# Two key tiles per attention cycle, value sums in SBUF, tiles turned by VectorE: a change to a fused attention and SwiGLU kernel

## The chip, the cores and the metric

The kernel runs on one core of one Trainium2 chip. The metric is device time in microseconds (us) of one execution; the median of several executions is compared. Beside the runs there is one profiled execution, whose trace gives the start and length of every instruction on the engines: PE (TensorE matmul), PEld (TensorE weight load), DVE (VectorE), ACT (ScalarE), POOL (GpSimd) and SP (SyncE, whose queue issues nearly all DMAs here).

## The reference

Two layers with the same weights; in each, an attention block and a feed-forward block are added to x. All values are float32; S = 2048 rows, D = 448, 16 query heads of 28 that share one key head and one value head, F = 1792.

```python
def _A_ref(x, wq, wk, wv, wo):            # H = 16, Dh = 28
    q = (x @ wq).reshape(B, S, H, Dh).transpose(0, 2, 1, 3)
    k = x @ wk                            # (B, S, 28)
    v = x @ wv
    scores = jnp.einsum("bhqd,bkd->bhqk", q, k) * (Dh ** -0.5)
    p = softmax(scores, axis=-1)
    o = jnp.einsum("bhqk,bkd->bhqd", p, v)
    return o.transpose(0, 2, 1, 3).reshape(B, S, H * Dh) @ wo

def _B_ref(x, w_gate, w_up, w_down):
    return (silu(x @ w_gate) * (x @ w_up)) @ w_down

for layer in range(2):
    x = x + _A_ref(_layernorm(x), wq, wk, wv, wo)
    x = x + _B_ref(_layernorm(x), w_gate, w_up, w_down)
```

## The kernel before, in words

**Data.** x stays in SBUF (`xres`, 16 tiles of 128 rows). The 2048 rows form four chunks of 512 (`c` = 0 to 3). Operands of the projections and of the feed-forward are split into a high and a low part in a rounded float32 (`split`, lines 133 to 135, on GpSimd), and products are summed in passes: high by high, low by high, high by low.

**Norm and transposes.** `norm_steps` (L210) gives one chunk's statistics and normalised tiles `xn` (L229 on VectorE; L230 copies the last 64 columns once more with GpSimd). `flip` (L241) turns four tiles at a time with TensorE transposes (L246); `flipped` takes them from PSUM: a copy (L252) and VectorE's subtraction (L253) into `xh` and `xl`. The last 64 of the 448 rows of the turned chunk stand twice, in both halves of the partitions. `rows3` (L128) loads weights in the same layout: one DMA for 384 rows, one that broadcasts the last 64 rows to both halves (L131).

**Projections.** 16 steps per layer (`project`, `q`): chunk by chunk, in each the four groups of columns in the order `TURN` = (3, 2, 0, 1) (L32). Groups 3 and 2 carry the keys in columns 112 to 127 and groups 0 and 1 the values; the queries go to DRAM and come back as stacked heads (`stack`, `parts`, `rows`: `qstack`). For the values VectorE turns the rows (L505) and GpSimd distributes them (`vsb`). In layer 0 the three first groups' `rows` DMAs (L323) are issued at step 13.

**Attention.** There are 16 groups per layer: a chunk of queries by four heads. For each group, 16 steps of one key tile (128 keys) each. `step(n)` (L557): 12 score matmuls (L565), three passes of four heads; heads 0 to 2 go into a tile of three banks (`threes[n % 2]`, two in turn), head 3 into bank 7 (`one`). ScalarE takes the exponential of `one` (L571) and then of the three banks (L572). Then TensorE does the value matmuls of the tile two steps earlier (`pv(n - 2)`, L602), which are summed in bank 6 over all 16 tiles; the ones column of `vsb` gives the row sums. At the end of a group, `post` (L610), called four steps after its last tile: VectorE copies bank 6 to SBUF (L615), four DMAs spread the row sums (`rs`, L618), and some steps later `rest` checks them (L624, L626), takes the reciprocal, sends it through DRAM (`rd`) back as a broadcast (`rb`), and GpSimd multiplies (L636) and splits into `onh`, `onl`. All engines keep the order in which the program is written.

**Between steps.** When a chunk's four groups are done, its out-projection follows in step 10 of a later group (`between_steps`, L575): 48 matmuls (L549) into the free tile of three banks and bank 7, and VectorE's sums into `xres`. In groups 8 and 12 chunk 0's transposes lie between them. In groups 5, 13 and 14 the norm of chunks 0, 1 and 2 is done one piece per step. The feed-forward's first weights are loaded during groups 11 to 13 (`weights`), with `rows3` too.

**Feed-forward.** 14 tiles of 128 columns of F, two at a time (`groups`, FG = 2); for each pair all four chunks. `unit` (L791) does gate and up (L292, 64-row matmuls side by side), ScalarE's silu (L825), VectorE's product (L826), the split of h (L827, L830), and in the next unit the down products, whose sums go to `xres` at the pair's end (`accumulate`, L743 on GpSimd). `rest` (L856) opens it: `turned(1)` flips chunk 1 on TensorE before the first unit of the second chunk, and `self.mid` puts the flips of chunks 2 and 3 into the middle of later units. Steps in `soon` are done so many units later. At the end of layer 0 the chunks are handed to layer 1's projections.

**The second version.** The program holds a second, safer version of everything (`full`), behind a branch that is taken only where row sums leave a range (`fine`). The profiled execution does not take it.

Of the kernel before, what the change touches and what calls it, by code (L numbers as in the profile page):

```python
# [8 lines left out]
F32 = mybir.dt.float32  # L9
# [6 lines left out]
P = 128  # L16
S = 2048
D = 448
# [13 lines left out]
TURN = (3, 2, 0, 1)  # L32
IDLE = 36
# [21 lines left out]
def forward(  # L55
# [72 lines left out]
    def rows3(dst, src, eng=nc.sync):  # L128
        n = src.shape[1]
        eng.dma_start(dst[:, 0:3], src[0:384, :].rearrange("(k p) n -> p k n", p=P))  # L130
        eng.dma_start(dst[:, 3], src[384:448, :][None].to_broadcast([2, 64, n]))  # L131
# [78 lines left out]
    def norm_steps(c, pool=pers):  # L210
# [14 lines left out]
        def apply(t):  # L225
# [4 lines left out]
            nc.gpsimd.tensor_copy(got["x"][:, t, D:512], o[:, 384:D])  # L230
# [18 lines left out]
    def flipped(tiles, k, pt, copy):  # L249
# [12 lines left out]
        nc.vector.tensor_tensor(xh[64:128, k, :], pt[64:128, :], high, ALU.subtract)  # L262

# [39 lines left out]
    class Attention:  # L303


        def __init__(self, layer):
# [3 lines left out]
            self.order = [(c, m) for c in range(NC) for m in TURN]  # L310
# [8 lines left out]
            for i in range(3):  # L319
                self.at(4 + 3 * i, lambda i=i: self.stack(i))  # L320
                self.at(6 + 3 * i, lambda i=i: self.parts(i))
                if not full:
                    self.at(13, lambda i=i: self.rows(i))  # L323
# [137 lines left out]
        def project(self):  # L461
# [5 lines left out]
            turned = [o[0] for o in self.order[self.seen : self.seen + 2] if o[1] == 3]  # L467
# [60 lines left out]
        def scores(self, ff):  # L528
            next(switch)
            with tc.tile_pool(name=f"at{self.layer}", bufs=1, reuse_waits="tile") as wp:  # L530
# [26 lines left out]
                def step(n):  # L557

                    i, kt = divmod(n, NT)
                    three, one = threes[n % 2], banks[7]  # L560
# [8 lines left out]
                    pt = wp.tile([P, 3, 512], F32, name="pt", bufs=3)  # L569
                    pt1 = wp.tile([P, 512], F32, name="pt1", bufs=2 if full else 3)  # L570
                    nc.scalar.activation(pt1, one, AF.Exp, scale=SCALE)  # L571
                    nc.scalar.activation(pt, three, AF.Exp, scale=SCALE)  # L572
                    pts[n] = [*(pt[:, j, :] for j in range(3)), pt1]

                def between_steps(n):  # L575

                    i, kt = divmod(n, NT)
                    free, one = threes[(n + 1) % 2], banks[7]
                    if full:
                        self.lent = free[:, 0, :]  # L580
                        self.advance(KC)
                        if kt == 11 and i + 1 < len(GR):
                            self.places[i + 1](free[:, 1, :])
                    if not todo or kt != 10:
                        return
                    c = todo.pop()
                    ks = list({8: (0, 1), 12: (2, 3)}.get(i, ()))
                    adds = []
                    for t in (1, 2, 3):
                        adds.append(outproj(c, t, free[:, t - 1, :]))  # L590
                        if ks:
                            flip(got, X0, [ks.pop(0)], one)
# [4 lines left out]
                def pv(n):  # L597
                    i, kt = divmod(n, NT)
                    if kt == 0:
                        accs[i] = banks[6]  # L600
                    for j in range(4):
                        nc.tensor.matmul(  # L602
                            accs[i][32 * j : 32 * j + 32, :], vsb[:, kt, :], pts[n][j],
                            start=(kt == 0), stop=(kt == NT - 1), skip_group_check=True,
                        )
                    del pts[n]
                    if kt == NT - 1:
                        due[n + 4] = post(i)

                def post(i):  # L610

                    c, g = GR[i]
                    out2 = halves("o2").bitcast(F32)
                    oraw, rb = out2[:, 0, :], out2[:, 1, :]
                    nc.vector.tensor_copy(oraw, accs.pop(i))  # L615
# [28 lines left out]
                fs, got = norm_steps(0)  # L644
                fs1, got1 = norm_steps(1)
                ff.norms[1] = got1
                ff.second = norm_steps(2)
                last = NT * len(GR)
                for n in range(last):
# [319 lines left out]
```

## Time and profile before

| | us |
|---|---|
| runs | 2038.59, 2038.96, 2035.05 (median 2038.59) |
| profiled execution | 2040.6 |
| its span in the trace | 2038.9 |
| mean granted TensorE clock | 0.996 of full speed |
| layer 0: start and projections | 0 to 72 |
| layer 0: attention (first to last exponentials) | 73 to 595 |
| layer 0: feed-forward | 596 to 1040 |
| layer 1: last projections | 1040 to 1081 |
| layer 1: attention | 1081 to 1600 |
| layer 1: feed-forward | 1601 to 2039 |

Busy time of the engines over the span:

```profile
PE 2015.1 (99%) x18613; PEld 1271.5 (62%) x18613; DVE 457.7 (22%) x890; ACT 1310.6 (64%) x2152; POOL 537.7 (26%) x601
PE   8999999999999999999999999999999999999998
ACT  3699798997973333333348997979979533333332
```

The first row gives each engine's busy time, its share of the span and the number of instructions. The other two cut the span into 40 slices of 51 us; each digit is the busy share of a slice in tenths. PE is busy in all of them. Matmuls are pipelined and their ends are modelled, so a busy PE is not PE at its peak: within attention it also waits for ScalarE and VectorE in ways that the busy share does not tell, and starts of instructions have to be read. ScalarE is near its limit in the two stretches of attention (slices 3 to 12 and 22 to 32, apart from those where the out-projections lie) and at a third elsewhere.

In the lines that follow, an instruction is given as start, length, engine, line, operation, tiles, shape and count; square brackets hold the idle time of the engine before it and what ended that.

### The profile page before, as it was taken

The page shows a single profiled execution, that of the slowest core. Times are in us where ns is not written, and L with a number is a line of the kernel's source. Part 1 is how long each engine was busy: PE and PEld are TensorE (multiplying, and loading weights), DVE is VectorE, ACT ScalarE, POOL GpSimd, SP SyncE. Part 2 cuts the span into 40 slices and gives each one's busy share as a digit, 9 for nine tenths or more (in the row PEclk, how much of TensorE's full clock was granted, in tenths as well). Part 3 has the DMA queues.
Part 4 walks back from the last instruction along what each step waited for, and adds up shares of the span by engine and source line. Part 5 has one row for each costly group of instructions (what it writes and reads, how often), then busy time and mean ns, then how long its engine had stood idle before and what let it go on. Part 6 is the DMA issues. An engine that isn't in the chain of part 4 may idle for free.

```text
span 2038.9 us, 43612 instructions
## 1 busy us (share of the span) xinstructions
PE 2015.1 (99%) x18613; PEld 1271.5 (62%) x18613; DVE 457.7 (22%) x890; ACT 1310.6 (64%) x2152; POOL 537.7 (26%) x601
## 2 busy tenths in 40 slices
PE   8999999999999999999999999999999999999998
PEld 6533434334348999999884334343343689988886
DVE  6200101001114323222461001010011242232322
ACT  3699798997973333333348997979979533333332
POOL 4313121021302333333441221111222123333320
PEclk9999999999999999999999999999999999999999
DMA  5201000011100111100031110000110000111101
GB/s 152 60 22 28 21 13 22 12 37 26 32 12 19 31 31 31 30 17 26 22 93 35 30 30 12 22 12 22 28 45 14 28 16 17 31 31 31 31 1 74
DMA packets 76512, 63.44 MB, mean 31 GB/s; under 512 B 22904, under 2 KB 63224, under 8 KB 76312
## 3 DMA queue, kind: packets, MB, share of 16 engines
q1 hardware_dynamic: 74820, 59.39, 10.4%
q8 instruction: 147, 2.41, 0.5%
q10 hardware_dynamic: 1492, 1.20, 0.2%
q14 instruction: 53, 0.43, 0.1%
HBM read 47.72 MB, written 12.32 MB: 29 GB/s over the span
## 4 chain that ended last, share of the span: by engine, by line
PE 50%; ACT 46%; issue 1%; DMA 1%; DVE 1%; SPq 0%; ACTq 0%; POOL 0%; DVEq 0%; POOLq 0%
PE bank L292 39%; ACT pt L572 31%; ACT pt L571 15%; PE bank L272 5%; PE three L549 2%; PE bank L549 2%; PE bank L246 1%; PE bank L602 0%; PE three L565 0%; DMA wr<-in_A_wk_dram 0%; PE bank L398 0%; DMA qstack<-rows 0%; DMA xres<-in_A_x_dram 0%; DVE xl L253 0%; DVE xn L229 0%
## 5 line engine op out<-in xcount | busy, mean ns | idle before, releaser
L572 ACT ACTIVATE pt<-three 128x1536 f32<-128x1536 f32 x512 | 741.1, 1447 | 0.0
L602 PE MATMUL bank<-pt,vsb 128*32 128x512 f32 x4096 | 546.0, 605 | 0.6 <-ACT pt L572 0.6
L565 PEld LDWEIGHTS three<-qstack,keys 32*128 32x128 f32 x4608 | 252.7, 183 | 450.6 <-ACT pt L571 393.6
L565 PE MATMUL three<-qstack,keys 32*128 32x512 f32 x4608 | 497.8, 425 | 4.1 <-DVE vt L505 2.3
L565 PE MATMUL bank<-qstack,keys 32*128 32x512 f32 x1536 | 492.6, 426 | 0.5 <-ACT pt L571 0.5
L292 PE MATMUL bank<-xh,wgh 64*128 64x512 f32 x1728 | 445.4, 390 | 0.4
L292 PE MATMUL bank<-xh,wgl 64*128 64x512 f32 x1404 | 366.8, 390 | 0.0
L571 ACT ACTIVATE pt<-bank 128x512 f32<-128x512 f32 x512 | 306.0, 598 | 71.6 <-PE bank L565 70.5
L292 PE MATMUL bank<-xl,wgh 64*128 64x512 f32 x1296 | 333.4, 390 | 0.0
L292 PE MATMUL bank<-wdh,h 64*128 64x448 f32 x1792 | 330.8, 364 | 1.5 <-ACT h L827 0.8
L292 PEld LDWEIGHTS bank<-xh,wgh 64*128 64x128 f32 x1728 | 260.9, 184 | 19.5 <-DVE xl L253 1.5
L743 POOL TENSOR_TENSOR xres<-stage,xres 128x448 f32<-128x448 f32 x108 | 127.7, 1204 | 497.8 <-ACT stage L742 497.8
L636 POOL TENSOR_TENSOR o<-o 128x512 f32<-128x512 f32 x32 | 41.1, 1284 | 820.4 <-DMA o<-rd 820.4
L292 PEld LDWEIGHTS bank<-wdh,h 64*128 64x128 f32 x1792 | 241.2, 184 | 15.8 <-issue 2.7
L565 PEld LDWEIGHTS bank<-qstack,keys 32*128 32x128 f32 x1536 | 243.9, 183 | 1.3 <-ACT pt L571 1.1
L299 ACT COPY seen<-bank 128x1 f32<-128x1 f32 x664 | 81.6, 163 | 247.8 <-PE bank L292 245.1
L292 PEld LDWEIGHTS bank<-xh,wgl 64*128 64x128 f32 x1404 | 215.1, 184 | 14.2
L292 PE MATMUL bank<-wdl,h 64*128 64x448 f32 x896 | 216.7, 366 | 0.0
L825 ACT ACTIVATE sg<-bank 128x512 f32<-128x512 f32 x112 | 67.3, 601 | 219.5 <-PE bank L292 214.4
L292 PEld LDWEIGHTS bank<-xl,wgh 64*128 64x128 f32 x1296 | 194.8, 184 | 10.5
L602 PEld LDWEIGHTS bank<-pt,vsb 128*32 128x32 f32 x4096 | 80.8, 108 | 189.9 <-issue 174.2
L826 DVE TENSOR_TENSOR sg<-bank,sg 128x512 f32<-128x512 f32 x112 | 77.5, 692 | 499.4 <-ACT sg L825 490.5
(115 smaller groups left out, 1732.1 us busy)
## 6 DMA issues: line engine op xcount, KB each, us to landing
o<-rd SPq DMA_DIRECT2D x32, 256.0 KB
qd<-stage SPq DMA_DIRECT2D x32, 224.0 KB
qraw<-qd SPq DMA_DIRECT2D x128, 56.0 KB
wdr<-in_B_w_down_dram SPq DMA_DIRECT2D x28, 224.0 KB
wr<-in_B_w_gate_dram SPq DMA_DIRECT2D x28, 192.0 KB
wr<-in_B_w_up_dram SPq DMA_DIRECT2D x28, 192.0 KB
out_dram<-xres SPq DMA_DIRECT2D x15, 224.0 KB
xres<-in_A_x_dram SPq DMA_DIRECT2D x3, 896.0 KB
```

Of the source, the lines that this page charges most:

```text
L272: nc.tensor.matmul(po, a, b, start=(i == 0), stop=(i == len(seq) - 1))
L292: nc.tensor.matmul(po, a, b, start=start, stop=stop, skip_group_check=True)
L299: nc.scalar.copy(seen[:, i : i + 1], po[:, 0:1])
L549: nc.tensor.matmul(po[:, 0:D], a[:, g, ts_], b[:, g, :], start=(g + z == 0), stop=(g == NG - 1 and z == 2))
L565: nc.tensor.matmul(three[:, j, :] if j < 3 else one, k[js, kp, ks], q[js, part, :], start=(z == 0), stop=(z == 2), tile_position=(32 * j, 0),)
L571: nc.scalar.activation(pt1, one, AF.Exp, scale=SCALE)
L572: nc.scalar.activation(pt, three, AF.Exp, scale=SCALE)
L602: nc.tensor.matmul(accs[i][32 * j : 32 * j + 32, :], vsb[:, kt, :], pts[n][j], start=(kt == 0), stop=(kt == NT - 1), skip_group_check=True,)
L636: nc.gpsimd.tensor_tensor(rb, oraw, rb, ALU.mult)
L743: nc.gpsimd.tensor_tensor(r, s, r, ALU.add)
L825: nc.scalar.activation(sg, pg[0], AF.Silu)
L826: nc.vector.tensor_tensor(sg, pg[1], sg, ALU.mult)
```

## The change

Lines of the changed kernel are meant where the tile or function is new.

**Attention.** A cycle takes two key tiles (`cycle(m)`, 128 cycles per layer). The first tile's head 3 goes into one single bank (`a`), the second's into the other (`b`); they swap roles each cycle (`singles`). ScalarE reads `a` and both tiles of three banks as before (L607, L608, L611); VectorE copies `b` to SBUF (L610), and ScalarE's fourth exponential works there in place (L612). The value matmuls of the cycle before (both tiles, 8 matmuls, L639) go into `a` once its exponential is taken, and VectorE copies (first cycle of a group, L646) or adds (L648) this into SBUF (`accs`). `rs` is asked for two cycles after the group's last sum (L659), the check and the reciprocal stand at L665 to L667. There are four `pt` and four `pt1` buffers.

**Small work.** Norm pieces come one per cycle (`aside`). For chunks 0 to 2 VectorE turns the normalised tiles in 32x32 blocks (`turn_tile`), four DMAs per tile put the blocks in place in DRAM, and `rows3` reads the turned chunk back. Chunk 0's halves are made by GpSimd during attention; chunk 1's by ScalarE and VectorE when the feed-forward opens, chunk 2's by GpSimd one unit later. TensorE still flips chunk 3. The out-projections come after the value matmuls of their cycle and hold no transposes.

**Projections and weights.** For the last chunk the order of the column groups is `LAST` = (1, 0, 2, 3), and the three first groups' `rows` are issued at steps 9, 11 and 13. `rows3` loads the last 64 rows with two DMAs, one for each half of the partitions.

```diff
+LAST = (1, 0, 2, 3)
...
     def rows3(dst, src, eng=nc.sync):
-        n = src.shape[1]
         eng.dma_start(dst[:, 0:3], src[0:384, :].rearrange("(k p) n -> p k n", p=P))
-        eng.dma_start(dst[:, 3], src[384:448, :][None].to_broadcast([2, 64, n]))
+        for half in (slice(0, 64), slice(64, 128)):
+            eng.dma_start(dst[half, 3], src[384:448, :])
...
+    def turn_tile(got, tb, raw, t):
+
+        nc.vector.transpose(tb[:, t, :], got["x"][:, t, 0:D])
+        to = raw.rearrange("(b d) (t g w) -> t g d b w", d=32, g=4, w=32)
+        for g in range(4):
+            nc.sync.dma_start(to[t, g], tb[32 * g : 32 * g + 32, t, :].rearrange("d (b w) -> d b w", w=32))
+
+    def halved(tiles, r, ks, copy, sub):
+
+        xh, xl, xd = tiles
+        for k in ks:
+            if k < 3:
+                copy(xh[:, k, :], r[:, k, :])
+                sub(xl[:, k, :], r[:, k, :], xh[:, k, :], ALU.subtract)
+                continue
...
-            self.order = [(c, m) for c in range(NC) for m in TURN]
+            self.order = [(c, m) for c in range(NC) for m in (TURN if c < NC - 1 else LAST)]
...
-                    self.at(13, lambda i=i: self.rows(i))
+                    self.at((9, 11, 13)[i], lambda i=i: self.rows(i))
...
+                def singles(m):
+
+                    return banks[6 + m % 2], banks[7 - m % 2]
+
+                def cycle(m):
+
+                    a, b = singles(m)
+                    pt, pt1 = tile_scores(2 * m, threes[0], a)
+                    nc.scalar.activation(pt1, a, AF.Exp, scale=SCALE)
+                    nc.scalar.activation(pt, threes[0], AF.Exp, scale=SCALE)
+                    pt, pt1 = tile_scores(2 * m + 1, threes[1], b)
+                    nc.vector.tensor_copy(pt1, b)
+                    nc.scalar.activation(pt, threes[1], AF.Exp, scale=SCALE)
+                    nc.scalar.activation(pt1, pt1, AF.Exp, scale=SCALE)
...
+                def pv(m, to):
+
+                    i, u = divmod(m, NT // 2)
+                    for y in range(2):
+                        n = 2 * m + y
+                        for j in range(4):
+                            nc.tensor.matmul(
+                                to[32 * j : 32 * j + 32, :], vsb[:, n % NT, :], pts[n][j],
+                                start=(y == 0), stop=(y == 1), skip_group_check=True,
+                            )
+                        del pts[n]
+                    if u == 0:
+                        accs[i] = halves("o2").bitcast(F32)
+                        nc.vector.tensor_copy(accs[i][:, 0, :], to)
+                    else:
+                        nc.vector.tensor_tensor(accs[i][:, 0, :], to, accs[i][:, 0, :], ALU.add)
+                    if u == NT // 2 - 1:
+                        due[m + 3] = post(i)
...
+                aside = {}
+                for c in range(NC - 1):
+                    fs, got = norm_steps(c, twice=False)
+                    ff.raw[c] = dram.tile([D, 512], F32, name=f"xt{self.layer}_{c}")
+                    m0 = NT // 2 * (4 * c + 5) + 3
+                    for n, f in enumerate(fs + turns(c, got)):
+                        aside[m0 + n + (n > 4)] = f
+                for n, f in enumerate(back()):
+                    aside[NT // 2 * 7 + 1 + n + (n > 0)] = f
+                aside[NT // 2 * 15 + 1] = lambda: ff.fetch(1)
...
+                    cycle(m)
+                    if m:
+                        pv(m - 1, singles(m)[0])
...
+                    if m in due:
+                        due.pop(m)()
+                    if m in aside:
+                        aside[m]()
+                    between_cycles(m)
+                pv(last - 1, banks[6])
...
+        def fetch(self, c):
+
+            self.got[c] = pers.tile([P, 4, 512], F32, name="xn")
+            rows3(self.got[c], self.raw[c])
+
+        def parts(self, c, copy, sub):
+
+            self.X[c] = xtile(self.xbp, self.xd[c])
+            halved(self.X[c], self.got.pop(c), range(4), copy, sub)
...
-            self.turned(1)
-            fs2, self.norms[2] = self.second
+            self.parts(1, nc.scalar.copy, nc.vector.tensor_tensor)
             fs3, self.norms[3] = norm_steps(3)
-            for f in fs2[5:] + fs3[:5]:
+            for f in fs3[:5]:
                 f()
+            self.fetch(2)
+            self.soon.append([0, lambda: self.parts(2, nc.gpsimd.tensor_copy, nc.gpsimd.tensor_tensor)])
             self.soon.append([1, lambda: [f() for f in fs3[5:]]])
-            for c in (2, 3):
-                self.mid[0, c - 1, 1] = [lambda c=c, ks=ks: self.turned(c, ks) for ks in ((0, 1), (2, 3))]
+            self.mid[0, 2, 1] = [lambda ks=ks: self.turned(3, ks) for ks in ((0, 1), (2, 3))]
```

117 lines of the change are left out of this document (53 added, 64 removed).

## The prediction

> **What bounds the kernel now.** I read the page, then the timeline of one steady stretch of attention, then the chain of waits at the stage borders. The page's chain gives the two layers of attention to ScalarE and the rest to TensorE:
>
> ```profile
> span 2038.9 us, 43612 instructions
> PE bank L292 39%; ACT pt L572 31%; ACT pt L571 15%; PE bank L272 5%; PE three L549 2%; PE bank L549 2%; PE bank L246 1%; PE bank L602 0%; PE three L565 0%; DMA wr<-in_A_wk_dram 0%; PE bank L398 0%; DMA qstack<-rows 0%; DMA xres<-in_A_x_dram 0%; DVE xl L253 0%; DVE xn L229 0%
> ```
>
> L572 and L571 are the exponentials; 46% of the span says that attention is theirs. The timeline says otherwise. First TensorE in one step (one key tile; columns: start, length, line, tiles; the 302.91 row is the second half of that step's four value matmuls), then ScalarE there and at the start of layer 1:
>
> ```profile
> 300.56 1.07 PE L602 MATMUL bank<-pt,vsb 128*32 128x512 f32 x8
> 301.56 0.50 PE L565 MATMUL three<-qstack,keys 32*128 32x512 f32 x3
> 301.90 0.40 PE L565 MATMUL three<-qstack,keys 32*128 32x512 f32 x3
> 302.13 0.40 PE L565 MATMUL three<-qstack,keys 32*128 32x512 f32 x3
> 302.91 0.61 PE L602 MATMUL bank<-pt,vsb 128*32 128x512 f32 x4
> 301.70 0.69 DVE L615 COPY o<-bank 128x512 f32<-128x512 f32 x1 [25.03 <-PE bank L602]
> 302.46 0.14 PEld L602 LDWEIGHTS bank<-pt,vsb 128*32 128x32 f32 x6 [0.36 <-DVE o L615]
> ```
> ```profile
> 300.74 0.60 ACT L571 ACTIVATE pt<-bank 128x512 f32<-128x512 f32 x1
> 302.65 0.60 ACT L571 ACTIVATE pt<-bank 128x512 f32<-128x512 f32 x1
> 1081.06 0.60 ACT L571 ACTIVATE pt<-bank 128x512 f32<-128x512 f32 x1 [0.76 <-PE bank L565]
> 1082.89 0.60 ACT L571 ACTIVATE pt<-bank 128x512 f32<-128x512 f32 x1
> ```
>
> TensorE repeats after 302.46 - 300.56 = 1.90 us. Inside: value matmuls to next scores 1.00 (two halves, 0.45 from 302.46 to 302.91 and 0.55), first to second score pass 0.34, second to third 0.23, third pass to value matmuls 0.33. A pass that follows one of its own kind costs 0.23; at each change between the two kinds some 0.1 is added, three times a step. ScalarE's pair of exponentials repeats after 1.91 here, but after 1.83 at 1081.06, where TensorE was ahead. So ScalarE could go 0.07 to 0.08 us faster, and TensorE with its changes sets the step: 512 steps of 1.90 are 973 us of the 2039. The chain names ScalarE because its instructions overlap so closely that no idle time is left to see.
>
> **The cycle.** The order of the changed program's instructions shows per cycle: scores of two tiles, then the value matmuls of the two tiles before, an eviction of one single bank by VectorE, and its sum into SBUF. TensorE alone then needs 1.00 + 2 x 0.45 for the value matmuls and 0.34 + 4 x 0.23 + 0.33 for the scores, 3.49 us against 3.80 for two steps. ScalarE needs 2 x 1.83 = 3.66 (the exponential that now reads SBUF has the same size; I take the same length, with 0.03 either way). Two loops of waits are new. ScalarE's: the single exponential frees the bank (0.60 and 0.06 to hand over), value matmuls 1.90, scores 0.34 + 0.23, and 0.52 from the third pass to the exponential (302.13 to 302.65): 3.65. VectorE's: the value matmuls go into a bank that the second tile's scores of the next cycle need, so those wait for the sum. Copies out of PSUM started 1.14 after a tile's value matmuls (300.56 to 301.70), so 1.14 + 0.90 for two tiles. For the sum itself I take the nearest row, VectorE's two-input instruction with one input in PSUM:
>
> ```profile
> L826 DVE TENSOR_TENSOR sg<-bank,sg x112: 691/692/693, 601.2 to 2026.7; 128x512 f32<-128x512 f32 x112
> L830 DVE TENSOR_TENSOR h<-sg,h x112: 691/693/1630, 602.6 to 2028.0; 128x512 fp32r<-128x512 f32 x112
> ```
>
> That is 0.69 (minimum, median and maximum agree), then 0.07 to TensorE (301.70 + 0.69 to 302.46), then the rest of the scores, 0.34 + 0.23 + 0.33. Sum: 2.04 + 0.69 + 0.07 + 0.90 = 3.70 us. This is the longest loop, and I forecast it: 0.10 under two steps, over 2 x 127 cycles **25 us less**. L830, with both inputs in SBUF, can take 1.63 instead of 0.69; if the sum did, the loop would be 4.64. The Trainium skill, "SBUF — State Buffer", section on the two separate sides, says that a VectorE instruction with two SBUF inputs and a GpSimd instruction lock each other out, and that others do not wait. L826 and L830 bear that out, and the sum has one SBUF input.
>
> Of what is queued behind the new waits: VectorE's eviction of the next cycle stands behind the sum and the cycle's small piece (statistics, a scaled tile, a turned tile, at most about 0.8). The sum ends 2.73 after the value matmuls, the eviction can start at about 3.8 and is needed only some 2 us later, so the pieces lie in that hole. If it is gone, each 0.1 us over it costs 0.1 us in that cycle.
>
> **Out-projection.** Three times a layer TensorE leaves the loop.
>
> ```profile
> 216.41 7.67 PE three L549 x36
> 228.50 0.60 ACT L571 ACTIVATE pt<-bank 128x512 f32<-128x512 f32 x1 [10.35 <-PE bank L565]
> 361.23 0.60 ACT L571 ACTIVATE pt<-bank 128x512 f32<-128x512 f32 x1 [11.04 <-PE bank L565]
> ```
>
> The two later times carry chunk 0's transposes, 0.69 more; they go, four times: 2.8 less. New: the value matmuls come before the 48 matmuls (7.67 x 48/36 = 10.2), not after, so nothing covers the last sum. From the value matmuls' start: 1.9 + 10.2 + about 0.8 for the sum with its hand-overs, then 0.34 + 0.23 + 0.52 to the exponential, 14.0; ScalarE's last work ends at 3.1; 10.9 idle against 10.35, six times: 3.3 more. **0.5 us more** in all.
>
> **The start.** The last 64 weight rows now go as two DMAs of 64 partitions instead of one that repeats its source.
>
> ```profile
> 5.76 9.54 DMA wr<-in_A_wk_dram
> GB/s 338 309 304 289 208 171 143 97 55 48 48 48 48 42 48 48 48 42 48 48 48 36 48 48 48 131 131 60 84 96 227 311 299 358 394 382 400 394 366 358
> 9.55 2.91 PE L246 MATMUL bank<-ident,xn 128*128 128x128 f32 x16 [2.08 <-DVE xn L229]
> 14.45 2.50 POOL L191 TENSOR_TENSOR wl<-wr,wh 128x896 fp32r<-128x896 f32 x2 [3.39 <-ACT wh L189]
> 16.21 0.79 PE L272 MATMUL bank<-xh,wh 128*128 128x512 f32 x1 [3.75 <-ACT xh L252]
> ```
>
> The GB/s row has 40 slices of 6.4 to 12.4 us: for some 2.5 us the repeating DMAs move 48 GB/s while 300 and more stand open. Spread, they land at about 8, the transposes' end (12.46) becomes the limit instead of 16.21, and GpSimd's low part follows. Bounds: nothing (they stay slow) and 4.2; I take the distance 16.21 - 12.46, **3.7 us less**. The later weights are loaded groups ahead and move nothing.
>
> **The start of attention.**
>
> ```profile
> 70.02 0.60 ACT stage L498
> 71.56 0.50 PE L565 MATMUL three<-qstack,keys 32*128 32x512 f32 x3 [2.06 <-DVE vt L505]
> 72.57 0.60 ACT L571 ACTIVATE pt<-bank 128x512 f32<-128x512 f32 x1 [1.96 <-PE bank L565]
> 83.13 0.60 ACT L571 ACTIVATE pt<-bank 128x512 f32<-128x512 f32 x1
> 66.00:96.00 30.00, 6.57 (x11) 0.89 0.16 48
> 1080.04 0.51 PE L565 MATMUL three<-qstack,keys 32*128 32x512 f32 x3 [1.76 <-DMA qstack<-rows]
> ```
>
> With the keys' projections last and the first rows loaded earlier, neither the turned values nor that DMA is late; next is ScalarE's last copy, which ends at 70.62. Layer 0 gains up to 72.57 - 70.64 = 1.9, layer 1 by the same step 0.7. In layer 0 the idle 2.06 us are followed by a granted clock of 0.89 (the row over 66 to 96 us, column after the count), and the first four steps take 83.13 - 72.57 = 10.56 instead of 7.6. With about 1 us of idle time I expect no drop, as after 1.76 in layer 1: 3.0 less. Together **5.6 us less**, between 0 and 6. The Trainium skill, "TensorE: Matmul & The Clock Gate", section on the clock gate, lets the clock fall after an idle window of about 3.4 us; the trace shows it after 2.06, so here the measurement decides.
>
> **The feed-forward.** It is TensorE's, so the transposes of chunks 1 and 2 count where they stood.
>
> ```profile
> 619.04 0.45 PE bank L246 x4
> 620.13 1.30 DVE xl L253 x2
> 621.47 10.08 PE bank L292 x81
> 631.55 1.03 PE bank L246 x8
> 634.00 1.02 PE bank L246 x8
> ```
>
> Chunk 1: TensorE stood from 619.04 to 621.47. VectorE's four subtractions still begin only behind the last out-projection sum, but the first matmul that needs one waits until about 620.5: 1.0 less. Chunk 2: 2.05 of transposes go; but its halves now come from GpSimd, behind a load of about 1 MB and two sums, and I find the last one 2 to 3 us late. I take nothing; bounds 2 less, 2 more. Over two layers **2 us less**.
>
> **Turned tiles.** VectorE's transposes lie in the hole above. Each tile issues four DMAs of 448 pieces of 128 bytes, and the row sums of a group (rs) are queued behind them. Nearest rows: a DMA of 128 such pieces (slices of 128.35 to 129.05 us) and one of 128 pieces of 64 bytes (115.05 to 115.40):
>
> ```profile
> GB/s 0 0 15 22 7 0 0 0 0 0 0 0 0 29 29 29 29 59 59 51 44 59 59 51 995 59 51 44 44 22 29 29 29 29 0 0 0 0 0 0
> GB/s 0 0 0 0 0 7 7 37 51 88 51 51 66 75 37 44 66 37 66 37 44 52 22 30 22 22 15 7 7 0 0 0 0 0 0 0 0 0 0 0
> DVE under L624 <- DMA rs<-o: 121.0, 30, 5.5
> ```
>
> They last 21 slices of 17.5 ns and 24 of 8.8 ns, 0.37 and 0.21 us, so 448 pieces take 0.7 to 1.3, four DMAs 2.9 to 5.2 against a cycle of 3.70. I take the lower, as the source has 32 partitions. At the upper, three cycles' DMAs leave rs some 5 us late. Today VectorE waits 121.0/30 = 4.0 us for rs about two steps after its DMAs; it now asks two cycles after, 3.6 us later. What is left lies in the hole. **Nothing.**
>
> **Sum.** 25 - 0.5 + 3.7 + 5.6 + 2 = 35.8 us less. The profiled execution took 2040.6 us, its span and 1.7 around it; less 36 that is 2004.8. The median of the runs is 2.0 lower, 2038.6: **2003 us**.
>
> **Rivals.** (1) ScalarE becomes the bound: the sum never delays the scores, because a pass begins earlier than I add up. Then the cycle is 3.66, 254 x 0.04 = 10 us less, and with luck at the start 1990. For: 3.65 to 3.70 lie close. Against: the rows of the sum are steady to 2 ns. (2) The cycle gains nothing: the change between score kinds of two tiles costs its 0.1 too, and the waiting scores add another, 3.80. Then 2028. For: the 0.1 is only seen with a wait or a change of kind beside it. Against: the passes within a tile show 0.23. (3) The pieces of 128 bytes hold rs up and VectorE, waiting for it, holds up its sums and so TensorE. At 2.4 us for a DMA, twice the upper row, twelve of them end about 11 us after the point at which four more would fit, rs comes 14 us after VectorE asks, 2 of it hidden: 12 us, three times a layer: 72 more, 2075. It turns the change to a loss from about 1.9 us a DMA. For: these write to HBM, which no row of that shape shows. Against: both rows are under 1.3. The Trainium skill, "DMA: Bandwidth & Descriptors", Specifications, says that below 512 bytes the DMA engines read, modify and write; it speaks for this rival, and no run shows it at 128 bytes to HBM in such number. That the change does not do what it says is ruled out by the order of its instructions.
>
> **Numbers.** Forecast 0.52 (1996 to 2012), rival 1 0.17 (1986 to 1996), rival 2 0.19 (2012 to 2034), rival 3 0.09, all else 0.03. The runs before spread by 0.19%, so 0.2%, 4 us, is what a measurement can tell from no change. Faster: 0.52 + 0.17 + 0.19 = 0.88 but for 0.01 at the edge, 0.87; same 0.03; slower 0.10. The range, 1986 to 2034, leaves out rival 3 and the tails.
>
> **What would show it.** Right: first single exponentials of successive cycles 3.70 us apart; before the second tile's scores a short wait on VectorE's sum; ScalarE with a gap of about 0.04 per cycle; the first projection matmul near 12.5 us; a clock of 1.00 at 66 to 96 us. Rival 1 shows 3.66 and no such wait. Rival 2 shows TensorE without gaps at 3.80. Rival 3 shows VectorE at L665 waiting for rs by many us. I am wrong if the single sums or evictions take longer than 0.69, or if the out-projections wait for GpSimd's normalised outputs.

## The result, and the profile after

The changed kernel takes **2002.41 us** (median of 4 runs, 2002.23 to 2003.07) against 2038.78 in the same comparison: a ratio of 0.9823, 95% interval 0.9808 to 0.9839. The forecast was 2003. The profiled execution took 2002.2 us, its span is 2000.5: 38.4 less than the span before.

From the page of the changed kernel, the chain by engine and by line:

```profile
PE 94%; DVE 2%; POOL 1%; ACT 1%; DMA 1%; issue 0%; ACTq 0%; POOLq 0%; SPq 0%; DVEq 0%
PE bank L318 39%; PE bank L639 24%; PE three L590 17%; PE bank L590 6%; PE bank L298 4%; PE three L575 2%; PE bank L575 2%; PE bank L248 1%; POOL xl L279 0%; DMA qd<-stage 0%; ACT pt L611 0%; DVE xn L230 0%; DMA xn<-xt 0%; DMA xres<-in_A_x_dram 0%; DVE xres L579 0%
```

The chain that gave attention to ScalarE before now gives it to TensorE (L639, L590). The experiments below show that before it named an engine whose work could shrink at no gain, and that after it hides ScalarE and VectorE, whose cuts together gain 43.5 us. What can be trusted is starts. One cycle in the timeline of the changed kernel (start, length, engine, line):

```profile
300.78 0.60 ACT L607 ACTIVATE pt<-bank 128x512 f32<-128x512 f32 x1
301.52 1.92 PE L639 MATMUL bank<-pt,vsb 128*32 128x512 f32 x16
303.38 0.50 PE L590 MATMUL three<-qstack,keys 32*128 32x512 f32 x3
303.57 0.69 DVE L648 TENSOR_TENSOR o<-bank,o 128x512 f32<-128x512 f32 x1 [1.25 <-PE bank L639]
303.93 0.64 ACT L612 ACTIVATE pt<-pt 128x512 f32<-128x512 f32 x1
304.12 0.19 PEld L590 LDWEIGHTS three<-qstack,keys 32*128 32x128 f32 x3 [0.21 <-ACT pt L611]
304.32 0.49 PE L590 MATMUL bank<-qstack,keys 32*128 32x512 f32 x1
304.47 0.60 ACT L607 ACTIVATE pt<-bank 128x512 f32<-128x512 f32 x1
305.20 1.92 PE L639 MATMUL bank<-pt,vsb 128*32 128x512 f32 x16
```

The single exponentials (L607) are 304.47 - 300.78 = 3.69 us apart. The loop that the prediction named fits link by link: value matmuls at 301.52, the sum 2.05 later, its 0.69, and 0.06 after its end (304.26) the second tile's single head (304.32), then 0.88 to the next value matmuls. Median of all cycles: 3.685. But the wait that the trace records there is for ScalarE: TensorE's weight loads wait 248 times for the exponential L611 (row 304.12) and never for the sum. Starts alone can't tell which of the two holds TensorE.

Where the 38.4 us of span went, from the starts in both traces (a stretch of attention runs from its first exponential to the end of its last):

| stretch | before | after | difference | forecast |
|---|---|---|---|---|
| to the first projection matmul | 16.21 | 12.29 | -3.9 | -3.7 |
| from there to layer 0's first exponential | 56.36 | 52.73 | -3.6 | -1.9 |
| attention of layer 0, slow clock at its start (from the trace of before: 10.56 for 7.6) | | | -3.0 | -3.0 |
| attention of layer 0, the rest | | | -14.4 | -12.25 |
| feed-forward of layer 0 and projections of layer 1 | 486.30 | 485.82 | -0.5 | -1.7 |
| attention of layer 1 | 519.13 | 504.82 | -14.3 | -12.25 |
| feed-forward of layer 1 | 438.68 | 440.06 | +1.4 | -1.0 |

The whole of layer 0's attention went from 522.19 to 504.79. The sum of the forecast column is the prediction's 35.8, but the parts that agree least, the projections and the feed-forward, have opposite signs.

### The profile page after: what moved, and what is told of

It reads as the page before. It is cut to its first block, busy times and chain, and to the rows that moved or that the text cites. A ratio compares the mean times of both kernels' runs of the same rounds, so it can differ in the third digit from the quotient of the medians.

```text
span 2000.5 us, 44597 instructions
## 1 busy us (share of the span) xinstructions
PE 1978.4 (99%) x18517; PEld 1337.5 (67%) x18517; DVE 785.4 (39%) x1370; ACT 1277.5 (64%) x2142; POOL 560.4 (28%) x611
## 4 chain that ended last, share of the span: by engine, by line
PE 94%; DVE 2%; POOL 1%; ACT 1%; DMA 1%; issue 0%; ACTq 0%; POOLq 0%; SPq 0%; DVEq 0%
PE bank L318 39%; PE bank L639 24%; PE three L590 17%; PE bank L590 6%; PE bank L298 4%; PE three L575 2%; PE bank L575 2%; PE bank L248 1%; POOL xl L279 0%; DMA qd<-stage 0%; ACT pt L611 0%; DVE xn L230 0%; DMA xn<-xt 0%; DMA xres<-in_A_x_dram 0%; DVE xres L579 0%
## 5 line engine op out<-in xcount | busy, mean ns | idle before, releaser
L639 PE MATMUL bank<-pt,vsb 128*32 128x512 f32 x4096 | 493.2, 598 | 0.5
L590 PE MATMUL bank<-qstack,keys 32*128 32x512 f32 x1536 | 483.8, 424 | 1.7 <-DVE xres L579 1.7
L590 PE MATMUL three<-qstack,keys 32*128 32x512 f32 x4608 | 448.8, 420 | 1.4 <-ACT stage L524 1.0
L590 PEld LDWEIGHTS three<-qstack,keys 32*128 32x128 f32 x4608 | 258.1, 182 | 282.2 <-ACT pt L608 185.2
L611 ACT ACTIVATE pt<-three 128x1536 f32<-128x1536 f32 x256 | 383.1, 1496 | 0.0
L608 ACT ACTIVATE pt<-three 128x1536 f32<-128x1536 f32 x256 | 379.4, 1482 | 0.0
L639 PEld LDWEIGHTS bank<-pt,vsb 128*32 128x32 f32 x4096 | 107.1, 109 | 249.1 <-issue 152.6
L648 DVE TENSOR_TENSOR o<-bank,o 128x512 f32<-128x512 f32 x224 | 155.0, 692 | 280.5 <-PE bank L639 276.4
L610 DVE COPY pt<-bank 128x512 f32<-128x512 f32 x256 | 176.9, 691 | 205.5 <-PE bank L590 203.1
L590 PEld LDWEIGHTS bank<-qstack,keys 32*128 32x128 f32 x1536 | 243.9, 183 | 7.8 <-DVE xres L579 3.6
```

What stands on the lines that cost most here:

```text
L590: nc.tensor.matmul(three[:, j, :] if j < 3 else one, k[js, kp, ks], q[js, part, :], start=(z == 0), stop=(z == 2), tile_position=(32 * j, 0),)
L608: nc.scalar.activation(pt, threes[0], AF.Exp, scale=SCALE)
L610: nc.vector.tensor_copy(pt1, b)
L611: nc.scalar.activation(pt, threes[1], AF.Exp, scale=SCALE)
L639: nc.tensor.matmul(to[32 * j : 32 * j + 32, :], vsb[:, n % NT, :], pts[n][j], start=(y == 0), stop=(y == 1), skip_group_check=True,)
L648: nc.vector.tensor_tensor(accs[i][:, 0, :], to, accs[i][:, 0, :], ALU.add)
```

## Experiments: what bounds the cycle

Three cuts of the changed kernel and one of the kernel before take half the columns out of an instruction. These kernels leave a part of the result out and serve for the time alone.

**half_sum**

```diff
-                        nc.vector.tensor_tensor(accs[i][:, 0, :], to, accs[i][:, 0, :], ALU.add)
+                        nc.vector.tensor_tensor(accs[i][:, 0, 0:256], to[:, 0:256], accs[i][:, 0, 0:256], ALU.add)
```

> The changed kernel, but VectorE's sum (L648) takes 256 of the 512 columns; the other 256 keep what the group's first two tiles gave. Theory 1 (VectorE's sum closes the longest loop, 3.69 us in the trace): the sum shrinks by about 0.25 us, and the next loop takes over, ScalarE's 3.65; 7 of 8 cycles gain 0.04, so 224 x 0.04 = 9 us less, 1993 to 1995. Theory 2 (ScalarE's own work of 3.65 to 3.69 bounds the cycle): no change, 2002, cycle 3.69. Theory 3 (TensorE without gaps): no change, 2002, cycle 3.69.

Measured: 2000.28 us (2 runs), ratio to before 0.9811 (0.9782 to 0.9839); median cycle 3.684. Neither 1994 nor quite 2002. ScalarE and the sum in its timeline:

```profile
300.38 0.70 ACT L607 ACTIVATE pt<-bank 128x512 f32<-128x512 f32 x1
300.87 1.55 ACT L608 ACTIVATE pt<-three 128x1536 f32<-128x1536 f32 x1
302.20 1.56 ACT L611 ACTIVATE pt<-three 128x1536 f32<-128x1536 f32 x1
303.18 0.42 DVE L648 TENSOR_TENSOR o<-bank,o 128x256 f32<-128x256 f32 x1 [1.31 <-PE bank L639]
303.54 0.75 ACT L612 ACTIVATE pt<-pt 128x512 f32<-128x512 f32 x1
304.07 0.70 ACT L607 ACTIVATE pt<-bank 128x512 f32<-128x512 f32 x1
```

The sum is 0.27 shorter, so VectorE's loop could go in about 3.42, yet the cycle stays at 304.07 - 300.38 = 3.69. Every exponential is now 0.1 longer than at the same place of the changed kernel (1.55 for 1.45, 0.70 for 0.60). I read this as an exponential that is issued early and queues behind its predecessor; in half_exp below, where ScalarE idles in each cycle, the exponentials of three banks keep 1.45 to 1.46. ScalarE is saturated, at 0.49 + 1.33 + 1.34 + 0.53 = 3.69, not at the 3.65 to 3.66 that was expected. The last step, from the exponential that reads SBUF to the next, is 0.53 where the other single exponential takes 0.49. The changed kernel itself shows the sign in part of its cycles: its L607 takes 0.60 to 0.70 us, 0.63 in the median, and 0.66 to 0.70 in most of the first twenty cycles.

**half_exp** (L607 on half the columns; the value matmuls read that half twice)

```diff
-                    nc.scalar.activation(pt1, a, AF.Exp, scale=SCALE)
+                    pts[2 * m][3] = pt1[:, None, 0:256].to_broadcast([P, 2, 256])
+                    nc.scalar.activation(pt1[:, 0:256], a[:, 0:256], AF.Exp, scale=SCALE)
```

> The changed kernel, but ScalarE's first exponential of a cycle (L607) takes 256 of the 512 columns, and the value matmuls read these twice. Theory 1 (VectorE's sum closes the longest loop): ScalarE has 0.25 us more slack, the cycle stays at 3.69, 2002. Theory 2 (ScalarE bounds the cycle): the cycle falls by 0.2 to 0.25 to TensorE's 3.49, 254 x 0.2 = 51 us less, 1951. Theory 3 (TensorE without gaps): no change, 2002.

Measured: 1999.73 us (2 runs), ratio 0.9808 (0.9780 to 0.9837); median cycle 3.685. Its lines are one further down, so L608 is the half exponential and L649 the sum:

```profile
300.11 0.38 ACT L608 ACTIVATE pt<-bank 128x256 f32<-128x256 f32 x1
302.91 0.69 DVE L649 TENSOR_TENSOR o<-bank,o 128x512 f32<-128x512 f32 x1 [1.25 <-PE bank L640]
303.65 0.18 PEld L590 LDWEIGHTS bank<-qstack,keys 32*128 32x128 f32 x1 [0.18 <-DVE o L649]
303.80 0.38 ACT L608 ACTIVATE pt<-bank 128x256 f32<-128x256 f32 x1
```

ScalarE has 0.22 us less to do, and the cycle is 303.80 - 300.11 = 3.69. So ScalarE alone is not the bound either. With ScalarE out of the way, TensorE's weight loads wait for the sum, 207 times in all (row 303.65, 0.05 after the sum's end): that is VectorE's loop. The 2 to 3 us that each cut gains are not in the steady cycle: each layer's attention is 0.7 to 0.8 us shorter, most of it at the out-projections and the first cycle behind them, and the rest is outside it.

**half_both** (both cuts)

> Both cuts: VectorE's sum and ScalarE's first exponential on 256 of 512 columns, value matmuls reading the half exponential twice. Theory 1: both loops fall below TensorE's own 3.49, so 7 of 8 cycles gain 0.20: 224 x 0.20 = 45 us less, 1957, although half_sum gains only 9 and half_exp nothing. Theory 2 (ScalarE bounds): the same as half_exp alone, 1951. Theory 3 (TensorE without gaps at 3.69): no change, 2002.

Measured: 1958.89 us (2 runs), ratio 0.9608 (0.9579 to 0.9637).

```profile
301.01 0.39 ACT L608 ACTIVATE pt<-bank 128x256 f32<-128x256 f32 x1
304.49 0.39 ACT L608 ACTIVATE pt<-bank 128x256 f32<-128x256 f32 x1
```

304.49 - 301.01 = 3.48 (median 3.485); 3.49 was forecast for TensorE. Single cuts gain 2.1 and 2.7 us, both together 43.5. That is the mark of two limits of the same length, VectorE's loop at 3.70 as summed up and ScalarE's work at 3.69. It also shows that in this cycle with half the changes of matmul kind TensorE needs at most 3.49 for two tiles. That 3.49 is TensorE's own time is not shown: ScalarE's steps with the half exponential, 0.28 + 1.33 + 1.33 + 0.53 = 3.47, are nearly as long.

**before_half_exp** (the kernel before; L571 on half the columns, and as in half_exp the value matmuls read them twice)

```diff
-                    nc.scalar.activation(pt1, one, AF.Exp, scale=SCALE)
+                    nc.scalar.activation(pt1[:, 0:256], one[:, 0:256], AF.Exp, scale=SCALE)
...
-                    pts[n] = [*(pt[:, j, :] for j in range(3)), pt1]
+                    pts[n] = [*(pt[:, j, :] for j in range(3)), pt1[:, None, 0:256].to_broadcast([P, 2, 256])]
```

> The kernel before, but the exponential of the single bank (L571) takes 256 of the 512 columns, and the value matmuls read these twice. My reading of the trace of before (TensorE with its changes of matmul kind sets the step of 1.90): no change, 2038. What the page's chain says (ScalarE's exponentials carry 46% of the span): the step falls with ScalarE's work, until TensorE without the 0.1 that each wait adds is the bound, 1.79: 512 x 0.11 = 56 us less, 1982.

Measured: 2038.80 us (8 runs) against 2038.61, ratio 0.9998 (0.9987 to 1.0009).

```profile
300.48 0.38 ACT L571 ACTIVATE pt<-bank 128x256 f32<-128x256 f32 x1 [0.19 <-PE bank L565]
302.37 0.38 ACT L571 ACTIVATE pt<-bank 128x256 f32<-128x256 f32 x1 [0.16 <-PE bank L565]
```

ScalarE now idles 0.16 to 0.19 us in every step, and the step is still 1.89. The chain's 46% for ScalarE named an engine whose work could shrink by 0.22 us a step at no gain.

## Experiments: the start and the clock

**weights_back** (the last weight rows by the repeating DMA again)

```diff
+        n = src.shape[1]
...
-        for half in (slice(0, 64), slice(64, 128)):
-            eng.dma_start(dst[half, 3], src[384:448, :])
+        eng.dma_start(dst[:, 3], src[384:448, :][None].to_broadcast([2, 64, n]))
```

> The changed kernel with the last 64 weight rows loaded as before, by one DMA that repeats its source. Theory (from the two traces): the first projection matmul goes back from 12.29 to about 16.2 us, 3.9 more, and with the idle time before it the granted clock falls to 0.5 and 0.74 for 8 us as it did in the trace of before, which costs about 3 more, while the 1.2 us wait for the low part of the weights that the changed kernel has at 14.21 goes: 3.9 + 3.0 - 1.0 = 5.9 us more, 2008. Rival (only the wait itself, no clock loss): 3.9 more, 2006. Rival (the gain came from elsewhere): 2002.

**order_back**

```diff
-LAST = (1, 0, 2, 3)
+LAST = TURN
...
-                    self.at((9, 11, 13)[i], lambda i=i: self.rows(i))
+                    self.at(13, lambda i=i: self.rows(i))
```

> The changed kernel with the last chunk's column groups in the old order and the three first groups' row DMAs at step 13 again. Theory: the turned values and the row DMA are late again: the first exponential of layer 0 1.9 us later, that of layer 1 1.3 later, and the granted clock falls after the idle 2 us in layer 0, which cost 3.0: 6.2 us more, 2008.5. Rival (the clock drop in the trace of before was the remainder of another idle time, not of this one): 3.2 more, 2005.5.

**before_start** (the kernel before with the two edits that these runs take back, and one line that finds the chunk to turn next fitted to the new order)

> The kernel before with the edits of the start alone: last weight rows as two DMAs, order (1, 0, 2, 3) for the last chunk, row DMAs at steps 9, 11 and 13; attention, transposes and feed-forward as before. Theory (the parts add up, by the two traces): first exponential 7.5 us earlier, the clock drop at 72 to 82 us gone (3.0), layer 1's first exponential 1.3 earlier: 11.8 less, 2027. Rival (the clock drop is not tied to these edits, as order_back kept the full clock after a longer idle time): 7.5 + 1.3 = 8.8 less, 2030. Rival (by weights_back and order_back the two parts are worth 3.6 and 3.3 by the medians): 6.9 less, 2032.

Measured: weights_back 2006.02 (4 runs; ratio 0.9836, 0.9819 to 0.9854), 3.6 more than the changed kernel; order_back 2005.70 (4 runs; 0.9845, 0.9823 to 0.9867), 3.3 more; before_start 2029.04 (5 runs; 0.9952, 0.9939 to 0.9966), 10.8 less than before in medians and 11.6 less in spans.

First the changed kernel's first projection matmuls and its first exponential; then the same of weights_back (its row by window: length, busy time and count of five engines, granted clock, DMA share, GB/s); then order_back:

```profile
12.29 0.50 PE L298 MATMUL bank<-xh,wh 128*128 128x512 f32 x1
14.21 0.50 PE L298 MATMUL bank<-xh,wl 128*128 128x512 f32 x1 [0.69 <-POOL wl L192]
65.02 0.61 ACT L607 ACTIVATE pt<-bank 128x512 f32<-128x512 f32 x1
```
```profile
16.44 0.79 PE L298 MATMUL bank<-xh,wh 128*128 128x512 f32 x1 [4.24 <-ACT xh L254]
16.00:20.00 4.00, 3.56 (x8) 2.60 (x9) 3.52 (x5) 2.89 (x6) 3.02 (x9) 0.57 0.78 262
69.42 0.61 ACT L607 ACTIVATE pt<-bank 128x512 f32<-128x512 f32 x1
```
```profile
66.50 0.50 PE L590 MATMUL three<-qstack,keys 32*128 32x512 f32 x3 [2.31 <-DMA qstack<-rows]
67.51 0.60 ACT L607 ACTIVATE pt<-bank 128x512 f32<-128x512 f32 x1 [2.21 <-PE bank L590]
```

weights_back puts the first matmul back by 16.44 - 12.29 = 4.2 us and the first exponential by 4.4; its span is 5.3 longer. The traced execution is the slowest of its four, so by span it lies near the theory's 5.9 and by the median nearer the first rival's 3.9; clock losses differ from run to run. Its matmuls run at a clock of 0.57 for one window of 4 us; in the kernel before it was longer:

```profile
16.20:20.20 4.00, 3.99 (x9) 2.87 (x10) 3.94 (x7) 2.46 (x5) 2.70 (x9) 0.50 0.73 238
20.20:24.20 4.00, 4.00 (x15) 3.19 (x14) 2.79 (x8) 1.07 (x2) 0.90 (x2) 0.74 0.23 66
```

There 4 us at 0.50 and 4 at 0.74 cost about 2 + 1 = 3 us. This explains the stretch from the first projection to attention, where the changed kernel gained 3.6 instead of 1.9: 3.0 of clock, less 1.2 for two new waits, 0.69 at 14.21, when the weights' high part is early and GpSimd's low part is late, and 0.49 at 26.67 for VectorE's `xl`. I had priced none of these.

Two DMAs do not make the early start sure. Of the nine traces with them, seven have the first projection matmul at 12.05 to 12.81 us, but half_both has it at 15.53 and pieces_twice at 14.65, because ScalarE there waits 2.03 and 1.83 us for the last weight rows, and the clock falls to 0.50 for 3.4 us at 16.76 and 16.26. The three traces with the repeating DMA have 16.21 to 16.44.

order_back shows that a clock drop is not a fixed price of an idle time: TensorE stood 2.31 us, longer than the 2.06 after which the kernel before fell to 0.89 over 30 us, and the clock stayed at 1.00. The rival of order_back was right for this trace; one of its four runs took 2010.79 us, and why is not known. In before_half_exp an idle time of 1.78 at the same place did bring the drop (0.50 at 72 to 74 us), and one of 1.87 before layer 1 too.

The traces show more. In each of them the clock is 1.00 or 0.50, and in one trace all its changes lie whole multiples of 3.413 us apart: in the kernel before it falls at 15.46 and at 73.49 us, 17 x 3.413 later, and is back at 80.32, 2 x 3.413 later. Cut into stretches of that length along these times (in order_back they are counted back from its fall at 618.19), the two idle times differ (kernel before, then order_back):

```profile
70.08:73.49 3.41, 1.46 (x19) 1.05 (x23) 0.83 (x2) 1.45 (x4) 2.63 (x10) 1.00 0.58 173
73.49:76.90 3.41, 3.41 (x17) 1.83 (x17) 0.21 (x1) 2.96 (x3) 1.09 (x1) 0.50 0.07 12
```
```profile
61.82:65.23 3.41, 2.37 (x11) 1.62 (x9) 2.88 (x6) 1.04 (x3) 0.23 (x1) 1.00 0.26 96
65.23:68.64 3.41, 2.14 (x26) 1.67 (x27) 1.13 (x2) 1.20 (x3) 2.86 (x10) 1.00 0.54 157
```

In the kernel before, one stretch holds 3.41 - 1.46 = 1.95 us without matmuls, and half clock follows. In order_back a border at 65.23 cuts the 2.31 us into 1.04 and 1.27, and nothing follows. In all twelve traces, from 12 us to 12 us before the end, the 23 stretches at full clock that half clock followed each held 1.44 us or more of idle time; of the others at full clock one alone held as much (1.76, before layer 1 in the kernel before). So in these traces it is the idle time within one stretch that counts; by these figures I estimate the border at 1.4 to 1.8 us. The Trainium skill, "TensorE: Matmul & The Clock Gate", section on the HAM clock gate, says that the activity window is free-running, so that the point of change moves from run to run. The 3.413 us between changes agree with that. No run here moved the phase on purpose.

In before_start all is at full clock, and its 11.6 us of span are near the theory's 11.8: what weights_back and order_back each bring back by the medians (3.6 + 3.3) leaves out clock losses that come and go.

## Experiments: chunk 2 and the turned tiles

The feed-forward was the step that came out worst. TensorE in the changed kernel when chunk 2's first unit begins (brackets: idle time and releaser), and the clock there in layers 0 and 1:

```profile
612.90 0.50 PE L318 MATMUL bank<-xl,wgh 64*128 64x512 f32 x2 [1.07 <-POOL xl L279]
614.24 0.50 PE L318 MATMUL bank<-xh,wgh 64*128 64x512 f32 x1 [0.60 <-POOL xh L286]
615.57 0.79 PE L318 MATMUL bank<-xh,wgh 64*128 64x512 f32 x1 [0.83 <-POOL xh L288]
```
```profile
612.00:617.00 5.00, 2.66 (x13) 1.77 (x15) 1.45 (x4) 0.28 (x2) 4.19 (x7) 0.81 0.02 7
617.00:622.00 5.00, 5.00 (x43) 4.59 (x41) 0.53 (x2) 1.09 (x6) 0.64 (x3) 0.85 0.00 0
```
```profile
1603.00:1608.00 5.00, 3.24 (x13) 2.16 (x15) 1.73 (x4) 0.32 (x2) 4.18 (x7) 0.70 0.00 0
1608.00:1613.00 5.00, 5.00 (x32) 4.26 (x31) 0.05 (x1) 0.45 (x4) 0.35 (x2) 0.62 0.00 0
```

In layer 0 that is three waits for GpSimd, 2.5 us in all (2.2 in layer 1), and behind them the clock: over the two windows of 5 us it costs 0.95 + 0.75 = 1.7 us in layer 0 and 1.5 + 1.9 = 3.4 in layer 1. This drop comes every time: all seven traces in which GpSimd makes these halves have it in both layers, and the two below in which it does not have none.

**chunk2_scalar**

```diff
-            self.soon.append([0, lambda: self.parts(2, nc.gpsimd.tensor_copy, nc.gpsimd.tensor_tensor)])
+            self.soon.append([0, lambda: self.parts(2, nc.scalar.copy, nc.vector.tensor_tensor)])
```

> The changed kernel, but chunk 2's halves are made by ScalarE (copies) and VectorE (subtractions) instead of GpSimd. Theory: in the changed kernel TensorE waits about 2.8 us for GpSimd's last halves and then runs at a granted clock of 0.85 and 0.62 for some 5 us, so that the feed-forward is 4.4 us (layer 0) and 5.6 us (layer 1) behind where it would be with the halves in time. ScalarE and VectorE have nothing to do for 4.4 us at that place, and need about 3 us: 10 us less, 1992.5. Rival (ScalarE's and VectorE's work delays the silu and its product by 1 to 2 us per layer): 6 to 8 less, 1995. Rival (the load of the turned chunk is the late one): no change, 2002.

Measured: 1994.55 us (4 runs), ratio to before 0.9788 (0.9771 to 0.9806); span 1991.9, 8.6 less than the changed kernel's. The waits for GpSimd and the clock drop are gone; one wait is new, in each layer:

```profile
607.61 0.50 PE L318 MATMUL bank<-xh,wgh 64*128 64x512 f32 x2 [0.89 <-ACT seen L325]
```

ScalarE's five copies in a row hold up its small `seen` copies, which TensorE waits for. That is the rival's kind of price, 1.2 us a layer.

**chunk2_split** (the edit against the changed kernel)

```diff
-        def parts(self, c, copy, sub):
+        def parts(self, c, copy, sub, ks=range(4)):
...
-            self.soon.append([0, lambda: self.parts(2, nc.gpsimd.tensor_copy, nc.gpsimd.tensor_tensor)])
+            copy, sub = nc.scalar.copy, nc.vector.tensor_tensor
+            self.soon.append([0, lambda: self.parts(2, copy, sub, range(2))])
+            self.mid[0, 1, 1] = [lambda k=k: self.parts(2, copy, sub, [k]) for k in (2, 3)]
```

> The kernel of chunk2_scalar, but only the first two pieces of chunk 2 are made one unit after the feed-forward opens; the other two are made inside the next unit, behind its small copies (seen). Theory (from the trace of chunk2_scalar): there ScalarE's five copies in a row hold up the small copies, TensorE waits 1.25 us for them in each layer, and nothing else is left of the delay; then 2 x 1.2 us go: 1994.55 - 2.4 = 1992. Rival (VectorE's subtractions between come late and the wait moves to the start of chunk 2's unit): no change against chunk2_scalar, 1994.5.

Measured: **1991.22 us** (5 runs), ratio to before 0.9767 (0.9754 to 0.9780), faster than both kernels; span 1988.9, 11.6 less than the changed kernel's, granted clock 1.00 in the mean. From 604 to 616 us TensorE is busy throughout, at full clock:

```profile
604.00:616.00 12.00, 12.00 (x112) 12.00 (x110) 7.23 (x11) 5.43 (x21) 3.91 (x6) 1.00 0.10 26
```

Counted from the end of layer 0's exponentials, the first silu of chunk 2 comes 46.5 us later (569.23 to 615.74), against 51.4 in the changed kernel (569.81 to 621.18) and 50.6 before (594.76 to 645.32); in layer 1 it is 46.5 against 52.7 and 50.6. The 4.9 + 6.1 us so gained are the 11.6 of span but for 0.6.

**pieces_twice** (each DMA of a turned tile issued twice)

```diff
-        for g in range(4):
+        for g in (0, 1, 2, 3, 0, 1, 2, 3):
```

> The changed kernel with every DMA of turned tiles (448 pieces of 128 bytes) issued twice. Theory (these DMAs lie in free queue time, and rs is asked for long after them): no change, 2002, within 0.1%. Rival (the pieces hold up rs and with it VectorE's sums): each tile's DMAs take twice as long, and for the 6 groups concerned rs comes later by the length of four DMAs or more, 2 to 5 us each, 10 to 30 us more.

Measured: 2014.76 us (4 runs, 2011.44 to 2018.31), ratio to before 0.9878 (0.9855 to 0.9902): 12.4 more than the changed kernel; the rival. Of the traced execution's 15.6 us of span, 3.0 lie before the first exponential, where its last weight rows were late, and 8.0 and 3.7 in the attention of the two layers. SP's queue and VectorE around one group's end, first in the changed kernel, then in this one (count at the end of a row, so 12 DMAs in 8.86 us):

```profile
405.71 8.86 SPq L271 DMA_DIRECT2D xt<-tb  x12
414.69 2.47 SPq L659 DMA_DIRECT2D rs<-o  x4
421.98 0.16 DVE L665 TENSOR_SCALAR under<-rs 128x16 f32<-128x16 f32 x1
```
```profile
411.47 14.52 SPq L271 DMA_DIRECT2D xt<-tb  x24
426.04 2.47 SPq L659 DMA_DIRECT2D rs<-o  x4
431.59 0.17 DVE L665 TENSOR_SCALAR under<-rs 128x16 f32<-128x16 f32 x1 [4.24 <-DMA rs<-o]
```

With 24 DMAs SP issues almost without a pause: 14.52 / 24 = 0.605 us each, 4.8 for a tile against a cycle of 3.69, so the row sums' DMAs fall behind and VectorE waits 4.24 us for them, and TensorE for VectorE; the clock is at 0.50 from 432.69 to 439.51. The DMA engines had room: from 411 to 426 us their busy share is 0.57. The row sums' DMAs land 431.59 - 428.51 = 3.1 us after their issue ends. In the changed kernel the issue ends at 417.16, so by this estimate they are there at about 420.2, 1.7 us before VectorE asks. A tile's four DMAs cost SP 2.4 us, inside the cycle. None of the 64 instructions of L665 in the changed kernel waits for the row sums. So nothing was lost, but the margin was small.

## Why the prediction was right, point by point

- **The bound before.** Right: before_half_exp shows that ScalarE's work did not set the step, though the chain said so.
- **The cycle.** Right in size (3.69 for 3.70), and half_exp and half_both bear the loop out. Incomplete in cause: ScalarE's 3.66 was mis-sized by 0.03, the price that I had named as a doubt for the exponential that reads SBUF. Its own time is 3.69, so rival 1's bound and the forecast's coincide. Neither sign of the loop is in the changed kernel's trace: not the gap of 0.04 on ScalarE, and not the wait for the sum, which only half_exp shows. The sums kept their 0.69 (at most 0.693 in 224, 61 of them beside an instruction of GpSimd). The Trainium skill, "SBUF — State Buffer", section on the two separate sides, also lists VectorE's two-port modes as waiting, so the prediction's "others do not wait" is wider than the page. No run here shows such a mode by name, and no term rests on it. Both layers together gained 28.7 us with the out-projections, where 25 - 0.5 was forecast: 0.11 per cycle for 0.10.
- **Out-projection.** 10.9 us of idle ScalarE were forecast for 10.35 and 11.04; the changed kernel has

```profile
215.95 0.60 ACT L607 ACTIVATE pt<-bank 128x512 f32<-128x512 f32 x1 [10.74 <-PE bank L590]
344.82 0.60 ACT L607 ACTIVATE pt<-bank 128x512 f32<-128x512 f32 x1 [10.75 <-PE bank L590]
```

  and no wait for GpSimd's outputs: the term of +0.5 is about 0.
- **The start.** Right for the first matmul of this trace (12.29 for 12.46), with some luck: two of the nine traces with the same start are 2.4 and 3.2 us later. Left out: the slow clock behind the late start in the trace of before (3.0) and two new waits (1.2).
- **The start of attention.** The 1.9 and the full clock (1.00 from 59 to 89 us) came as forecast. But that this idle time costs 3.0 was too firm: order_back, with 2.31 cut in two by the border of a stretch, kept the clock.
- **The feed-forward.** Chunk 1 right: 1.1 us a layer for 1.0. Chunk 2 is the step that failed: I saw that GpSimd's last half comes 2 to 3 us late and booked it against the transposes as nothing. The clock drop behind the wait was not in it, although the same trace showed one after 2.06 us. Net of the transposes that it saves, the chunk costs 2.0 us in layer 0 and 3.2 in layer 1; with the halves in time it would have gained 2.9 in each.
- **Turned tiles.** Right that they cost nothing here. Wrong in the resource: SP's issue, 0.6 us a DMA, is what ran out in pieces_twice, with the DMA engines at 0.57. Rival 3's mechanism is real, and begins between one and two times the DMAs.

By the medians the total was hit within 1 us, by the spans within 2.6 (38.4 against 35.8). The missed gain of the projections and the cycles (1.7 + 4.2) and the missed loss of the feed-forward and what follows it (1.2 + 2.4) cancel in good part. So the close hit of the total is partly luck, and its terms are the better measure.

## What to carry to other kernels

Where two loops through different engines have nearly the same length, cutting either shows nothing: cut both at once before an engine is called free, and read starts and lengthened instructions rather than the chain, which names whichever engine has no visible gap. When an operation is taken off the busiest engine and given to a slow one, price the wait for the last piece together with the clock drop that can follow the idle time, and give the work to the engines that stand idle at that very place, in pieces small enough not to block what they are waited for. DMAs on one queue are counted by their issue time, and the question is who stands behind them.

## What was not expected of the hardware

- An exponential of 128x512 took 0.64 us when it read SBUF and 0.60 when it read a PSUM bank, and held up the next one by 0.53 instead of 0.49.
- Idle times of TensorE of 1.76 to 2.31 us were followed by the half clock in some places and by none in others; what counted was, with one exception, how much of them fell into one of the stretches of 3.41 us at whose ends the clock changes. Of the 4.9 and 6.1 us by which chunk 2's first silu comes later than in chunk2_split, 2.5 and 2.2 are waits, 1.7 and 3.4 are slow clock behind them, and 0.7 and 0.5 are not accounted for.
